# Running sum of the log decay by triangular matmul instead of a vector scan, with decay logits and values loaded token-major

## The chip, the cores and the metric

The kernel runs on one core of one Trainium2 chip. The metric is the device time of one execution, in microseconds (us). Engines are named as in the profile: PE (TensorE), PEld (its weight loads), DVE (VectorE), ACT (ScalarE), POOL (GpSimd), SP (SyncE, which here only issues DMAs).

## What is computed

A gated linear attention over 4 batches, 8 heads, 768 tokens and head size 48 feeds a mixture of 8 experts with a greedy, capacity-bound assignment, and that feeds a two-layer network with the nonlinearity h * cos(h). The change lies in the attention:

```python
f = 1.0 / (1.0 + np.exp(-f_logit))
for t in range(S):
    state = f[:, :, t, :, None] * state + np.einsum('bhd,bhe->bhde', k[:, :, t], v[:, :, t])
    y[:, :, t] = np.einsum('bhd,bhde->bhe', q[:, :, t], state)
```

## The kernel before

The program has three stages in a row: attention, a search of routing thresholds, and the experts with the two-layer network behind them. The attention stage takes the recurrence in chunks of 128 tokens. With 4 batches and 6 chunks there are 24 units u, u = 4 * chunk + batch. The 8 heads of a unit are held as 4 pairs; one head of a pair lies on partitions 0 to 47, the other on 64 to 111, and the rest is padding.

For a unit, `forget` makes l = ln(1 + exp(-f_logit)) on ACT, which is minus the log of the decay. `decay` makes its running sum A over the 128 tokens, on DVE, by one scan over 4 pairs x 128 tokens (L259); a second operand, `amask`, is 0 at each pair's first token, which restarts the sum, and a limit elsewhere. `scale` makes exp(A) and exp(-A) on ACT (L266, L267), the last column of the latter into G (L268), and scales keys and queries with them on POOL into kT (L270) and qT (L272). `turn` transposes kT on PE (L278). `scores` multiplies keys and queries on PE (L289), `cut` masks the scores on DVE (m, L293). `mix` adds state times queries (L303) and values times masked scores (L305) on PE and copies the sum to yT on ACT (L307). `outer` makes the chunk's own keys times values on PE (L316), `carry` adds them to the state on DVE (L326, L328), `fade` scales the state with G on POOL (L334). `gate` turns yT to token-major and makes the router logits in one product xl on PE (L341); ACT copies the rows out (L346), DVE sums the logits (L352). After every fourth unit `first_counts` runs a row of small DVE instructions (`best_expert`, L189 to L196, and L205) and four matmuls cn (L211), which start the search.

A loop over i spreads a unit over five turns: `at(k, f)` runs step f of unit i - k. Each engine keeps the order in which the program is written (`in_order`), so within a turn DVE runs carry, conversions, cuts, scan; PE runs xl, transposes, products, scores, outer products; ACT runs the copy of xl, the copy of the transposed keys, the exponentials, yT, and then the two activations of `forget`. Beside this, a generator converts the two-layer network's weights in 28 parts, about eight of its steps in each turn (`fill`): a load on SP (wr), an Abs on ACT (wv, L132), integer operations on DVE (L150, L152, L154, and w, L159), a rounding copy on ACT (wih and woh, L166), and a subtraction on DVE (L136).

Loads are issued on SP two turns ahead. q, k and f come together, feature-major, into one of three ring buffers (two DMAs of 48 partitions); v comes token-major, padded to 64 columns a head. `warm_up` runs bf16 matmuls on zeros at the end of turns 0 and 2 (18 and 12 of them).

The two tiles `cn0` and `tot` and the warming tile have a PSUM bank of their own (tag `sm`); with `w`, `tr`, `tk`, `sc0`, `sc1`, `y` and `kv` all eight banks are taken.

Of the kernel before, what the change touches and what calls it, by code (L numbers as in the profile page):

```python
# [9 lines left out]
F32 = mybir.dt.float32  # L10
# [3 lines left out]
AF = mybir.ActivationFunctionType  # L14
ALU = mybir.AluOpType
# [4 lines left out]
P = 128  # L20
B, H, S, D = 4, 8, 768, 48
HD = H * D
NCH = S // P
NU = B * NCH
NP = H // 2
E = 8
# [3 lines left out]
DECAY_LIMIT = 60.0  # L30
# [168 lines left out]
def first_counts(nc, wk, ps, K, Z, a, n):  # L199
    V = nc.vector  # L200
    s = slice(a, a + n)
    C = wk.tile([P, n, P], BF16, name="C0", tag="C0")

    def reach():
        V.tensor_tensor(C, Z["mx"][:, s, None].to_broadcast([P, n, P]), K["t0"].bitcast(F32)[:, None, :].to_broadcast([P, n, P]), op=ALU.is_ge)  # L205

    best_expert(nc, wk, K, Z["lg"][:, s], Z["mx"][:, s], Z["wm"][:, s], Z["oh"][:, s], n, reach)
    yield
    cn = ps.tile([P, E], F32, name="cn0", tag="sm")
    for c in range(n):  # L210
        nc.tensor.matmul(cn, C[:, c], Z["oh"][:, a + c], start=(c == 0), stop=(c == n - 1))  # L211
    if a == 0:
        V.tensor_copy(Z["cn"], cn)
    else:
        V.tensor_tensor(Z["cn"], Z["cn"], cn, op=ALU.add)
    yield


def attention(tc, nc, ctx, K, qkf, v64, xs, Z, G, wp, wg, win, wout, consts, late):
    V, SC, PE, GP = nc.vector, nc.scalar, nc.tensor, nc.gpsimd  # L220
    ap = ctx.enter_context(tc.tile_pool(name="at", bufs=1))
    wk = ctx.enter_context(tc.tile_pool(name="wk", bufs=2))
    ps = ctx.enter_context(tc.tile_pool(name="aps", bufs=1, space=PSUM))
    warm = ap.tile([P, 512], BF16, name="warm")
    V.memset(warm, 0.0)
    ring = [ap.tile([P, 3, NP, P], F32, name=f"ring{i}") for i in range(3)]
    for t in ring:
        V.memset(t[:, 2], 60.0)
        GP.memset(t[:, :2], 0.0)
    consts()  # L230
    amask = ap.tile([P, NP, P], F32, name="amask")
    V.memset(amask, DECAY_LIMIT + 2.0)
    V.memset(amask[:, :, 0:1], 0.0)
    st_all = [ap.tile([P, NP, P], F32, name=f"st{b}") for b in range(B)]
    for t in st_all:
        GP.memset(t, 0.0)
    st = {}

    def load(u):
        if u < NU:  # L240
            c, b = divmod(u, B)
            x = ring[u % 3]
            for a, z in ((2, 3), (0, 2)) if u == 0 else ((0, 3),):
                for j in range(2):
                    nc.sync.dma_start(x[64 * j:64 * j + D, a:z], qkf[b, c, j, :, a:z])
            v = wk.tile([P, H, 64], F32, name="v", tag="v", bufs=6)
            nc.sync.dma_start(v, v64[b, c * P:(c + 1) * P])
            st[u] = dict(x=x, v=v)

    def forget(u):  # L250
        x = st[u]["x"]
        uu = wk.tile([P, NP * P], F32, name="uu", tag="uu", bufs=1)
        SC.activation(uu, x[:, 2].rearrange("p a t -> p (a t)"), AF.Exp, scale=-1.0)
        SC.activation(uu, uu, AF.Ln, bias=K["ones"][:, 0:1])
        st[u]["l"] = uu

    def decay(u):
        A = st[u]["A"] = wk.tile([P, NP, P], F32, name="A", tag="A")
        V.tensor_tensor_scan(A.rearrange("p a t -> p (a t)"), amask.rearrange("p a t -> p (a t)"), st[u].pop("l"), 0.0, op0=ALU.min, op1=ALU.add)  # L259

    def scale(u):
        d = st[u]
# [33 lines left out]
    def mix(u):  # L296
        c, b = divmod(u, B)
        d = st[u]
        T, v = st_all[b], d["v"]
        y = ps.tile([P, NP, P], F32, name="y", tag="y")  # L300
        for p in range(NP):
            if c > 0:
                PE.matmul(y[:, p], T[:, p], d["qT"][:, p], start=True, stop=False)  # L303
            for j in range(2):
                PE.matmul(y[64 * j:64 * j + 64, p], v[:, 2 * p + j], d["sc"][j][:, p], start=(c == 0), stop=True)  # L305
        yT = d["yT"] = wk.tile([P, NP, P], F32, name="yT", tag="yT")
        SC.copy(yT, y)  # L307

    def outer(u):
        if u // B < NCH - 1:  # L310
            d = st[u]
            kv = d["kv"] = ps.tile([P, NP, D], F32, name="kv", tag="kv")
            for p in range(NP):
                for j in range(2):
                    h = 2 * p + j
                    PE.matmul(kv[64 * j:64 * j + D, p], d["kk"][:, p, 64 * j:64 * j + D], d["v"][:, h, :D], start=True, stop=True)  # L316

    def carry(u):
        c, b = divmod(u, B)
# [38 lines left out]
            yield from first_counts(nc, wk, ps, K, Z, u - n + 1, n)  # L358

    def warm_up(n):  # L360
        w = ps.tile([P, 512], F32, name="wp", tag="sm")
        for _ in range(n):
            PE.matmul(w, warm[:, :P], warm, start=True, stop=True)

# [16 lines left out]
    for i in range(NU + 5):  # L381
        def at(k, f, *a):
            if 0 <= i - k < NU:
                f(i - k, *a)

        def fill(n):
            for _ in range(n):
                next(conv, None)
        counts, gates = gates, gate(i - 4) if 0 <= i - 4 < NU else iter(())
        if i > NU:  # L390
            next(tail, None)
        at(4, carry)
        next(gates, None)
        at(2, turn)
        at(1, scale)
        F = (3, 2, 3) if i > 1 else (0, 0, 0)
        fill(F[0])
        at(3, mix)
        at(0, forget)
        next(counts, None)  # L400
        next(gates, None)
        fill(F[1])
        at(2, scores)
        fill(F[2])
        at(2, cut, 0)
        at(2, cut, 1)
        at(0, decay)
        next(gates, None)
        at(4, fade)
        at(3, outer)  # L410
        fill(0 if i < NU else 3)
        if i < len(WARM) and WARM[i]:
            warm_up(WARM[i])
        if i == 0:
            turning()
        load(i + 2)
# [433 lines left out]


@with_exitstack
def kernel(ctx, tc, qkf, v64, qkvf, wg, wcat, win, wout, out):
    nc = tc.nc
    V = nc.vector
    cp = ctx.enter_context(tc.tile_pool(name="cp", bufs=1))
# [18 lines left out]
    def late(ps):  # L875
# [1 line left out]
        cnt = cp.tile([P, 1], F32, name="cnt")  # L877
        V.tensor_scalar(ok, G.rearrange("p a b -> p (a b)"), math.exp(-DECAY_LIMIT), 0.0, op0=ALU.is_ge, op1=ALU.add, accum_out=cnt)
        yield
        tot = ps.tile([1, 1], F32, name="tot", tag="sm")  # L880
        nc.tensor.matmul(tot, cnt, K["ones"][:, 0:1], start=True, stop=True)
        V.tensor_copy(flag, tot)
        yield
# [2 lines left out]

    with ExitStack() as actx:
        with in_order(tc, nc):
            R = attention(tc, nc, actx, K, qkf, v64, xs, Z, G, wp, wg, win, wout, consts, late)
    with ExitStack() as fctx:  # L890
        sp = fctx.enter_context(tc.tile_pool(name="sp", bufs=1))
        pools = recurrence_pools(tc, fctx)
# [9 lines left out]
        experts(tc, nc, ectx, K, R, Z, xs, wcat, out)  # L902


_INS = ["qkf", "v64", "qkvf", "wg", "wcat", "win", "wout"]
_OUTS = [((B * S, HD), "float32")]


def layout(q, k, v, f_logit, moe_w_gate, moe_w1, moe_w2, moe2_w_in, moe2_w_out):
# [2 lines left out]
    tok = [a.transpose(0, 2, 1, 3).reshape(B, S, HD) for a in (q, k, v, f_logit)]  # L912
    w1 = moe_w1.reshape(E, 3, P, F1 // P, P).transpose(0, 2, 3, 1, 4).reshape(E, P, F1 // P, HD)
    w2 = moe_w2.reshape(E, F1 // P, P, HD).transpose(0, 2, 1, 3)
    dmaj = [a.reshape(B, NP, 2, NCH, P, D).transpose(0, 3, 2, 5, 1, 4) for a in (q, k, f_logit)]
    got = {
        "qkf": np.stack(dmaj, 4), "v64": np.pad(v.transpose(0, 2, 1, 3), ((0, 0), (0, 0), (0, 0), (0, 64 - D))), "qkvf": np.stack(tok, 2), "wg": moe_w_gate, "wcat": np.concatenate([w1, w2], 3),
        "win": moe2_w_in, "wout": moe2_w_out,
    }
    got = {n: np.ascontiguousarray(a) for n, a in got.items()}  # L920
# [24 lines left out]
```

## Time and profile before

| What | us |
|---|---|
| Median of 3 runs | 911.61 |
| Lowest and highest run | 911.2, 913.1 |
| Span of the profiled execution, from first to last instruction | 909.6 |
| PE busy, share of the span | 828.2, 91% |
| DVE busy | 648.3, 71% |
| ACT busy | 371.4, 41% |
| POOL busy | 394.4, 43% |

The profiled execution's own time is not listed apart from the three runs; its span of 909.6 us is 1.6 us under the lowest of them and 2.0 us under the median. The shares are means over stages with different limits, so what matters is read by stage. Matmuls are pipelined and their ends are modelled: PE's pace is read from start to start. In rows in order of time, the bracket at the end holds the idle time before the instruction and what ended it; x is how many instructions a row merges, and an fp32 matmul has two records. In rows of a group, the two numbers behind the bar are busy us and mean ns of one.

### The profile page before, as it was taken

How to read it: one execution, taken by the hardware profiler on the slowest of the kernel's cores; microseconds unless marked ns; L12 is line 12 of the kernel's file. 1: busy time of each engine (PE TensorE's matmuls, PEld its weight loads, DVE VectorE, ACT ScalarE, POOL GpSimd, SP SyncE). 2: the span in 40 equal slices, each digit the busy share in tenths (PEclk: the TensorE clock that was granted, in tenths of full speed). 3: DMA queues.
4: the chain of work that ended last, by engine and by line, in shares of the span. 5: the costliest groups of instructions: out<-in, count | busy, mean ns of one | idle time of the engine just before them, and what ended most of it. 6: DMA issues, size and time to landing. Idle time of an engine off the chain costs nothing.

```text
span 909.6 us, 15391 instructions
## 1 busy us (share of the span) xinstructions
PE 828.2 (91%) x5672; PEld 753.7 (83%) x5674; DVE 648.3 (71%) x1521; ACT 371.4 (41%) x686; POOL 394.4 (43%) x326
## 2 busy tenths in 40 slices
PE   6688889885399999999999999999999999999996
PEld 3566657664299998998999899989989999999996
DVE  7899999997657946975695588469756945653453
ACT  4646656551133352343235233423532352533332
POOL 4444544440341472365138324723651474634133
PEclk9889999987589999999999999999999999999999
DMA  8987777820320230122013002301220133200000
GB/s 198 232 200 193 184 186 174 197 83 28 102 67 1 79 107 8 53 54 87 1 53 114 27 1 79 113 3 53 62 78 1 53 114 90 74 29 27 1 1 27
DMA packets 27331, 73.45 MB, mean 81 GB/s; under 512 B 4624, under 2 KB 7696, under 8 KB 27248
## 3 DMA queue, kind: packets, MB, share of 16 engines
q1 hardware_dynamic: 24176, 62.95, 26.1%
q0 software_dynamic: 3072, 9.44, 3.2%
q8 instruction: 46, 0.75, 0.3%
q14 instruction: 37, 0.30, 0.1%
HBM read 62.94 MB, written 9.44 MB: 80 GB/s over the span
## 4 chain that ended last, share of the span: by engine, by line
PE 66%; DVE 5%; issue 1%; DMA 1%; POOL 0%; SPq 0%; POOLq 0%; ACT 0%; DVEq 0%
PE pC L698 7%; PE accD L761 7%; PE pC L699 7%; PE accD L763 7%; PE pC L700 7%; PE accD L762 7%; PE pA L698 4%; PE pA L699 3%; PE accB L698 3%; PE pA L700 3%; PE accB L699 3%; PE accB L700 3%; DVE C L508 2%; PE cn L504 1%; DVE thr L556 1%; DVE thr L548 1%
## 5 line engine op out<-in xcount | busy, mean ns | idle before, releaser
L751 POOL TENSOR_TENSOR gl<-g,gh 128x384 fp32r<-128x384 f32 x128 | 134.5, 1052 | 266.2 <-ACT gh L750 263.2
L681 POOL TENSOR_TENSOR wl<-raw,wh 128x768 fp32r<-128x768 f32 x64 | 118.2, 1853 | 41.1 <-ACT wh L680 40.5
L761 PE MATMUL accD<-woh,gh 128*128 128x384 f32 x384 | 131.0, 341 | 0.0
L763 PE MATMUL accD<-woh,gl 128*128 128x384 f32 x384 | 130.4, 340 | 0.5 <-POOL gl L751 0.5
L700 PE MATMUL pC<-yTh,wil 128*128 128x384 f32 x384 | 130.1, 339 | 0.0
L762 PE MATMUL accD<-wol,gh 128*128 128x384 f32 x384 | 129.4, 337 | 0.0
L699 PE MATMUL pC<-yTl,wih 128*128 128x384 f32 x384 | 129.4, 337 | 0.0
L698 PE MATMUL pC<-yTh,wih 128*128 128x384 f32 x384 | 129.0, 339 | 0.0
L745 ACT ACTIVATE fr<-fr,halfpi 128x384 f32<-128x384 f32 x128 | 78.8, 616 | 105.2 <-DVE fr L744 97.6
L747 DVE TENSOR_TENSOR g<-pC,fr 128x384 f32<-128x384 f32 x128 | 71.0, 555 | 61.8 <-ACT fr L745 55.0
L750 ACT CAST gh<-g 128x384 fp32r<-128x384 f32 x128 | 65.8, 514 | 112.8 <-DVE g L747 99.8
L742 DVE TENSOR_SCALAR ki<-pC 128x384 int32<-128x384 f32 x128 | 70.8, 553 | 20.6 <-PE pC L700 19.8
L690 DVE SCALAR_TENSOR_TENSOR hl<-pA,hh 128x384 fp32r<-128x384 f32 x64 | 35.5, 555 | 65.4 <-ACT hh L689 65.2
L270 POOL TENSOR_TENSOR kT<-ring,em 128x512 f32<-128x512 f32 x24 | 33.1, 1381 | 104.8 <-ACT em L266 104.8
L680 ACT CAST wh<-raw 128x768 fp32r<-128x768 f32 x64 | 52.6, 833 | 62.8 <-DMA raw<-in_wcat_dram 29.6
L689 ACT ACTIVATE hh<-pA 128x384 fp32r<-128x384 f32 x64 | 31.5, 492 | 112.6 <-PE pA L700 112.6
L763 PEld LDWEIGHTS accD<-woh,gl 128*128 128x128 f32 x384 | 72.0, 188 | 1.6 <-POOL gl L751 1.1
L744 DVE SCALAR_TENSOR_TENSOR fr<-pC,ki 128x384 f32<-128x384 f32 x128 | 71.1, 556 | 3.1
L699 PEld LDWEIGHTS pC<-yTl,wih 128*128 128x128 f32 x384 | 72.1, 188 | 0.5 <-DVE yTl L693 0.5
L761 PEld LDWEIGHTS accD<-woh,gh 128*128 128x128 f32 x384 | 72.1, 188 | 0.1
L762 PEld LDWEIGHTS accD<-wol,gh 128*128 128x128 f32 x384 | 72.2, 188 | 0.0
L700 PEld LDWEIGHTS pC<-yTh,wil 128*128 128x128 f32 x384 | 72.1, 188 | 0.1
(178 smaller groups left out, 1818.9 us busy)
## 6 DMA issues: line engine op xcount, KB each, us to landing
raw<-in_wcat_dram SPq DMA_DIRECT2D x64, 384.0 KB, 3.3
ring<-in_qkf_dram SPq DMA_DIRECT2D x46, 288.0 KB, 5.8
v<-in_v_dram SPq DMA_DIRECT2D x24, 256.0 KB, 6.2
wr<-in_win_dram SPq DMA_DIRECT2D x12, 512.0 KB, 5.4
wr<-in_wout_dram SPq DMA_DIRECT2D x16, 384.0 KB, 3.5
xs<-xx SPq DMA_DIRECT2D x24, 192.0 KB, 5.4
ring<-in_qkf_dram SPq DMA_DIRECT2D x2, 192.0 KB, 3.6
xg<-xs,idx POOLq DMA_INDIRECT x24
```

The source lines that it names most:

```text
L681: GP.tensor_tensor(l, raw, h.bitcast(F32), op=ALU.subtract)
L698: PE.matmul(o, ah, bh, start=first, stop=False)
L699: PE.matmul(o, ah, bl, start=False, stop=False)
L700: PE.matmul(o, al, bh, start=False, stop=last)
L742: V.tensor_scalar(ki, p, INV2PI, 0.25, op0=ALU.mult, op1=ALU.add)
L744: V.scalar_tensor_tensor(fr, p, INV2PI, ki, op0=ALU.mult, op1=ALU.subtract)
L745: SC.activation(fr, fr, AF.Sin, bias=halfpi, scale=TWO_PI)
L747: V.tensor_tensor(g, p, fr, op=ALU.mult)
L751: GP.tensor_tensor(gl, g, gh.bitcast(F32), op=ALU.subtract)
L761: PE.matmul(r["accD"][t], gh[:, s], R["oh"][:, f], start=(f == 0), stop=False)
L762: PE.matmul(r["accD"][t], gh[:, s], R["ol"][:, f], start=False, stop=False)
L763: PE.matmul(r["accD"][t], gl[:, s], R["oh"][:, f], start=False, stop=(f == NF - 1))
```

## The change

The running sum moves from DVE to PE: with l token-major, four fp32 matmuls per unit (one for each pair, l as weights, the 0/1 triangle `mask` as the moving operand) give A feature-major in PSUM. f is therefore loaded token-major, together with v, which loses its padding: one DMA of 128 partitions from the token-major array that the fallback path had already. The ring buffers hold q and k alone. For unit 0 f is loaded first, then q and k, then v. `logs` are two padded tiles whose padding stays 0. The limit that `amask` put on A is gone. The products with v are 48 instead of 64 columns wide, and the padding rows of their PSUM tile are zeroed once. A takes the bank `sm`; what was in it moves to the bank of `kv`. `decay` is called at the end of a turn, behind `outer`, and ahead of the warming matmuls.

```diff
-    cn = ps.tile([P, E], F32, name="cn0", tag="sm")
+    cn = ps.tile([P, E], F32, name="cn0", tag="kv")
...
-    ring = [ap.tile([P, 3, NP, P], F32, name=f"ring{i}") for i in range(3)]
+    ring = [ap.tile([P, 2, NP, P], F32, name=f"ring{i}") for i in range(3)]
     for t in ring:
-        V.memset(t[:, 2], 60.0)
-        GP.memset(t[:, :2], 0.0)
+        GP.memset(t, 0.0)
+    logs = [ap.tile([P, NP, 2, 64], F32, name=f"logs{i}") for i in range(2)]
+    for t in logs:
+        V.memset(t, 0.0)
+    yps = ps.tile([P, NP, P], F32, name="y", tag="y")
+    V.memset(yps, 0.0)
     consts()
-    amask = ap.tile([P, NP, P], F32, name="amask")
-    V.memset(amask, DECAY_LIMIT + 2.0)
-    V.memset(amask[:, :, 0:1], 0.0)
...
-            for a, z in ((2, 3), (0, 2)) if u == 0 else ((0, 3),):
-                for j in range(2):
-                    nc.sync.dma_start(x[64 * j:64 * j + D, a:z], qkf[b, c, j, :, a:z])
-            v = wk.tile([P, H, 64], F32, name="v", tag="v", bufs=6)
-            nc.sync.dma_start(v, v64[b, c * P:(c + 1) * P])
-            st[u] = dict(x=x, v=v)
+            vf = wk.tile([P, 2, HD], F32, name="vf", tag="vf", bufs=6)
+            src = qkvf[b, c * P:(c + 1) * P, 2:4]
+            if u == 0:
+                nc.sync.dma_start(vf[:, 1], src[:, 1])
+            else:
+                nc.sync.dma_start(vf, src)
+            for j in range(2):
+                nc.sync.dma_start(x[64 * j:64 * j + D], qk[b, c, j])
+            if u == 0:
+                nc.sync.dma_start(vf[:, 0], src[:, 0])
+            st[u] = dict(x=x, v=vf[:, 0].rearrange("t (h d) -> t h d", h=H), f=vf[:, 1])
 
     def forget(u):
-        x = st[u]["x"]
-        uu = wk.tile([P, NP * P], F32, name="uu", tag="uu", bufs=1)
-        SC.activation(uu, x[:, 2].rearrange("p a t -> p (a t)"), AF.Exp, scale=-1.0)
-        SC.activation(uu, uu, AF.Ln, bias=K["ones"][:, 0:1])
-        st[u]["l"] = uu
+        uu = wk.tile([P, NP, 2, D], F32, name="uu", tag="uu", bufs=1)
+        SC.activation(uu.rearrange("t p j d -> t (p j d)"), st[u]["f"], AF.Exp, scale=-1.0)
+        SC.activation(logs[u % 2][:, :, :, :D], uu, AF.Ln, bias=K["ones"][:, 0:1])
 
     def decay(u):
-        A = st[u]["A"] = wk.tile([P, NP, P], F32, name="A", tag="A")
-        V.tensor_tensor_scan(A.rearrange("p a t -> p (a t)"), amask.rearrange("p a t -> p (a t)"), st[u].pop("l"), 0.0, op0=ALU.min, op1=ALU.add)
+        A = st[u]["A"] = ps.tile([P, NP, P], F32, name="A", tag="A")
+        for p in range(NP):
+            PE.matmul(A[:, p], logs[u % 2][:, p].rearrange("t j d -> t (j d)"), K["mask"], start=True, stop=True)
...
-                PE.matmul(y[64 * j:64 * j + 64, p], v[:, 2 * p + j], d["sc"][j][:, p], start=(c == 0), stop=True)
+                PE.matmul(y[64 * j:64 * j + D, p], v[:, 2 * p + j], d["sc"][j][:, p], start=(c == 0), stop=True)
...
-        w = ps.tile([P, 512], F32, name="wp", tag="sm")
+        w = ps.tile([P, 512], F32, name="wp", tag="kv")
...
         at(2, cut, 1)
-        at(0, decay)
         next(gates, None)
         at(4, fade)
         at(3, outer)
+        at(0, decay)
         fill(0 if i < NU else 3)
         if i < len(WARM) and WARM[i]:
             warm_up(WARM[i])
```

On PE, between one turn's last scores and the next turn's products, with a state (sc are the scores, kv the outer products, tk the transposed keys, st the state), the order before was

```order
L289 MATMUL sc_664<-qT,kT 128x128
L316 MATMUL kv<-v,kk 48x48 x8
L341 MATMUL xl<-turn,yT 128x104 x4
L278 MATMUL tk<-ident,kT 128x128 x4
L303 MATMUL y<-qT,st_138 128x128
L305 MATMUL y<-m,v 64x128 x2
```

and is now

```order
L294 MATMUL sc_679<-qT,kT 128x128
L321 MATMUL kv<-vf,kk 48x48 x8
L264 MATMUL A<-mask,logs_93 128x128 x4
L346 MATMUL xl<-turn,yT 128x104 x4
L283 MATMUL tk<-ident,kT 128x128 x4
L308 MATMUL y<-qT,st_138 128x128
L310 MATMUL y<-m,vf 48x128 x2
```

Four matmuls of A stand between the outer products and the next turn's xl; all else keeps its place.

On DVE, around the cuts of a turn (m) and the carry of the next (st), the order before was

```order
L293 TENSOR_TENSOR m<-sc_407,mask 128x512
L293 TENSOR_TENSOR m<-sc_408,mask 128x512
L259 SCALAR_TENSOR_TENSOR A<-amask,uu 128x512
L328 COPY st_138<-kv 48x4x48 x2
L152 TENSOR_SCALAR wv<-wv 128x512
L154 SCALAR_TENSOR_TENSOR wv<-wr,wv 128x512
```

and is now

```order
L298 TENSOR_TENSOR m<-sc_416,mask 128x512
L298 TENSOR_TENSOR m<-sc_417,mask 128x512
L333 COPY st_138<-kv 48x4x48 x2
L152 TENSOR_SCALAR wv<-wv 128x512
L154 SCALAR_TENSOR_TENSOR wv<-wr,wv 128x512
```

The scan is gone from between them, and the carry follows the cuts.

## Rows read from the trace of the kernel before

**Rows 1.** Page, DVE's busy tenths in 40 slices of the span.
```profile
DVE  7899999997657946975695588469756945653453
```

**Rows 2.** Stretches: length, PE, PEld, DVE, ACT, POOL busy (instructions), PEclk, DMA share, GB/s.
```profile
45.99:196.00 150.01, 126.53 (x1204) 95.42 (x1202) 146.69 (x240) 89.60 (x181) 71.11 (x54) 0.90 0.73 180
...
131.97:138.16 6.19, 6.19 (x39) 4.29 (x39) 5.97 (x15) 3.90 (x8) 3.57 (x3) 0.51 0.69 183
...
250.00:909.60 659.60, 642.14 (x3927) 617.48 (x3927) 424.44 (x1080) 245.41 (x435) 291.23 (x235) 0.99 0.16 50
```

**Rows 3.** Waits, 0 to 230 us: who waited for whom, us in total, times, longest.
```profile
POOL kT L270 <- ACT em L266: 104.8, 24, 8.5
PEld y L305 <- DVE m L293: 27.7, 36, 2.4
ACT em L266 <- DVE A L259: 25.7, 17, 3.7
...
ACT wih L166 <- DVE w L159: 13.6, 7, 2.9
```

**Rows 4.** Groups by line on DVE, 45.99 to 197.22 us.
```profile
L259 DVE TENSOR_TENSOR_SCAN A<-amask,uu 128x512 f32<-128x512 f32 x19 | 23.1, 1214 | 0.0
```

**Rows 5.** PE in order of time, one step: start us, us, instruction, count.
```profile
110.46 1.16 PE L289 MATMUL sc<-qT,kT 64*128 64x128 f32 x16
111.55 0.56 PE L316 MATMUL kv<-v,kk 128*48 128x48 f32 x16
112.05 1.14 PE L341 MATMUL xl<-turn,yT 128*128 128x104 f32 x8
113.02 0.60 PE L278 MATMUL tk<-ident,kT 128*128 128x128 f32 x4
113.46 0.39 PE L303 MATMUL y<-qT,st 128*128 128x128 f32 x2
...
115.23 0.49 PE L303 MATMUL y<-qT,st 128*128 128x128 f32 x2
115.65 0.44 PE L305 MATMUL y<-m,v 128*64 128x128 f32 x4
116.02 0.49 PE L303 MATMUL y<-qT,st 128*128 128x128 f32 x2
```

**Rows 6.** ACT in the same step, in order of time.
```profile
110.58 0.58 ACT L307 COPY yT<-y 128x512 f32<-128x512 f32 x1 [1.32 <-PE y L305]
...
111.72 0.72 ACT L254 ACTIVATE uu<-uu,ones 128x512 f32<-128x512 f32 x1
```

**Rows 7.** DVE in order of time: first of a count, and the carry behind.
```profile
132.60 0.16 DVE L189 TENSOR_REDUCE mx<-lg 128x4 f32<-128x32 f32 x1
...
134.79 0.71 DVE L326 TENSOR_TENSOR st<-st,kv 48x192 f32<-48x192 f32 x2
```

**Rows 8.** PE and DVE in order of time, head of the program.
```profile
1.28 6.27 PE L363 MATMUL wp<-warm 128*128 128x512 bf16 x18 [1.28 <-DVE warm L225]
...
16.10 0.43 DVE L150 TENSOR_SCALAR wv<-wv 128x512 f32<-128x512 f32 x1 [1.87 <-ACT wv L132]
```

**Rows 9.** DVE, three conversions in time; three lines' shortest, median, longest (ns).
```profile
125.53 1.21 DVE L150 TENSOR_SCALAR wv<-wv 128x384 f32<-128x384 f32 x1
126.78 1.31 DVE L152 TENSOR_SCALAR wv<-wv 128x384 int32<-128x384 int32 x1
128.12 1.17 DVE L154 SCALAR_TENSOR_TENSOR wv<-wr,wv 128x384 int32<-128x384 int32 x1
...
L150 DVE TENSOR_SCALAR wv<-wv x28: 344/428/1495, 16.1 to 206.6; 128x384 f32<-128x384 f32 x16, 128x512 f32<-128x512 f32 x12
L152 DVE TENSOR_SCALAR wv<-wv x28: 359/887/1383, 16.6 to 207.0; 128x384 int32<-128x384 int32 x16, 128x512 int32<-128x512 int32 x12
L154 DVE SCALAR_TENSOR_TENSOR wv<-wr,wv x28: 548/693/1805, 18.0 to 207.4; 128x384 int32<-128x384 int32 x16, 128x512 int32<-128x512 int32 x12
```

**Rows 10.** PE in order of time, the wait before its clock fell.
```profile
131.01 0.43 PE L305 MATMUL y<-m,v 128*64 128x128 f32 x2 [1.79 <-DVE m L293]
```

More of the change, by code (lines that the diff above doesn't have):

```diff
@@ L216, in first_counts, with attention @@
     yield
-def attention(tc, nc, ctx, K, qkf, v64, xs, Z, G, wp, wg, win, wout, consts, late):
+def attention(tc, nc, ctx, K, qk, qkvf, xs, Z, G, wp, wg, win, wout, consts, late):
     V, SC, PE, GP = nc.vector, nc.scalar, nc.tensor, nc.gpsimd
@@ L299, in mix @@
         T, v = st_all[b], d["v"]
-        y = ps.tile([P, NP, P], F32, name="y", tag="y")
+        y = yps
         for p in range(NP):
@@ L315, in outer @@
                     h = 2 * p + j
-                    PE.matmul(kv[64 * j:64 * j + D, p], d["kk"][:, p, 64 * j:64 * j + D], d["v"][:, h, :D], start=True, stop=True)
+                    PE.matmul(kv[64 * j:64 * j + D, p], d["kk"][:, p, 64 * j:64 * j + D], d["v"][:, h], start=True, stop=True)
     def carry(u):
@@ L852, with kernel @@
 @with_exitstack
-def kernel(ctx, tc, qkf, v64, qkvf, wg, wcat, win, wout, out):
+def kernel(ctx, tc, qk, qkvf, wg, wcat, win, wout, out):
     nc = tc.nc
@@ L879, in late @@
         yield
-        tot = ps.tile([1, 1], F32, name="tot", tag="sm")
+        tot = ps.tile([1, 1], F32, name="tot", tag="kv")
         nc.tensor.matmul(tot, cnt, K["ones"][:, 0:1], start=True, stop=True)
@@ L888 @@
         with in_order(tc, nc):
-            R = attention(tc, nc, actx, K, qkf, v64, xs, Z, G, wp, wg, win, wout, consts, late)
+            R = attention(tc, nc, actx, K, qk, qkvf, xs, Z, G, wp, wg, win, wout, consts, late)
     with ExitStack() as fctx:
@@ L902 @@
         experts(tc, nc, ectx, K, R, Z, xs, wcat, out)
-_INS = ["qkf", "v64", "qkvf", "wg", "wcat", "win", "wout"]
+_INS = ["qk", "qkvf", "wg", "wcat", "win", "wout"]
 _OUTS = [((B * S, HD), "float32")]
@@ L914, in layout @@
     w2 = moe_w2.reshape(E, F1 // P, P, HD).transpose(0, 2, 1, 3)
-    dmaj = [a.reshape(B, NP, 2, NCH, P, D).transpose(0, 3, 2, 5, 1, 4) for a in (q, k, f_logit)]
+    dmaj = [a.reshape(B, NP, 2, NCH, P, D).transpose(0, 3, 2, 5, 1, 4) for a in (q, k)]
     got = {
-        "qkf": np.stack(dmaj, 4), "v64": np.pad(v.transpose(0, 2, 1, 3), ((0, 0), (0, 0), (0, 0), (0, 64 - D))), "qkvf": np.stack(tok, 2), "wg": moe_w_gate, "wcat": np.concatenate([w1, w2], 3),
+        "qk": np.stack(dmaj, 4), "qkvf": np.stack(tok, 2), "wg": moe_w_gate, "wcat": np.concatenate([w1, w2], 3),
         "win": moe2_w_in, "wout": moe2_w_out,
```

## The prediction

> **What bounds the kernel now.** I read the slices of the page first, then the stretches, then the waits, then one step in time. In the slices of 22.7 us each, VectorE (DVE) stands at 9 from the second to the ninth and falls off behind that [rows 1]: that is the attention stage, the only one that the change touches. The stretches give numbers [rows 2]: between the scan that starts at 45.99 us and the one at 196.00 lie 18 steps (19 scans, the group in [rows 4]), so a step takes 150.01 / 18 = 8.33 us. DVE is busy for 146.69 us of it, 8.15 us a step or 97.8%. PE is busy for 126.53 at a mean granted clock of 0.90, ACT for 89.60, POOL for 71.11. From 250 us on, in the experts, PE is busy for 642.14 of 659.60 us, and nothing in that stretch is edited.
>
> The waits say the same from the other side [rows 3]: PE's weight loads wait for the masked scores m of DVE (27.7 us), ACT for A from the scan (25.7 us) and for w of the weight conversion (13.6 us). No wait of that length has DVE as the one that waits. What DVE sheds in this stage is therefore time, until another engine's own work per step is reached. The question is how close that is.
>
> **The change, part by part.**
>
> *The scan goes.* In these 18 steps it costs 23.1 / 19 = 1.21 us each [rows 4]. DVE's work falls from 8.15 to 6.94 us a step, and at the same 97.8% a step that only DVE bounds would take 7.09.
>
> *Four matmuls a step come to PE.* First PE's own work, from a step at the full clock [rows 5]: scores 1.09 us (110.46 to 111.55), outer products 0.50, xl 0.97, transposes 0.44, and four pairs of state and score product of 0.79 each (115.23 to 116.02), 3.16: together 6.16. The trace has no fp32 matmul with the triangle. The nearest below is the transpose, 128x128 against 128 columns, 0.44 us for four; the nearest above is the state product L303, 0.42 us each (115.23 to 115.65), 1.68 for four, which sits between matmuls of another tile shape. I take xl, 0.97 us: it too is four fp32 matmuls in a row with 128x128 weights, with two records each, only with 104 columns for 128. PE then needs 6.16 + 0.97 = 7.13 us (6.60 to 7.84 by the ends), still below 8.33, but no longer with room.
>
> *A wait comes with them.* The matmul of step u needs the logarithm of step u, and ACT takes Exp and Ln only after the copy yT, which needs the last product on PE. Today yT starts at 110.58, and Ln runs from 111.72 to 112.44 [rows 6]. Both activations shrink from 512 to 384 columns, together by at most a quarter of twice 0.72, 0.36 us; I take 0.2, since part of each is fixed: the end is 112.24. PE is through with the outer products at 112.05 [rows 5]. So it waits some 0.2 us in each step, and xl, transposes and the products of the next step are queued behind that. The loop from product to yT, logarithm, matmul and next product takes 7.13 + 0.2 = 7.33 us. ACT itself has 89.60 us of work in 150 and bounds nothing; that em and ep now read from PSUM is taken as nothing.
>
> *The steps that count.* After every fourth step DVE runs best_expert in a row, from 132.60 to the carry at 134.79, 2.19 us [rows 7]. Averaged that is 0.55, so DVE has 6.39 us in a plain step and 8.58 in a counting one, 8.77 with the same 2.2% idle. PE bounds the plain steps and DVE the counting ones. The masks can be late by the length of the new matmul without PE noticing, but ACT's rounding copies, too, wait for DVE ahead of yT, so I credit no carry-over: (3 x 7.33 + 8.77) / 4 = 7.69 us. With full carry-over it would be 7.33.
>
> *The head.* The first matmul of A now stands before the 18 warming matmuls on PE, which ran from 1.28 us for 6.27 [rows 8]. It must wait for the first load and logarithm, so warming ends later by that much, and the first transposes are behind it. The cover is DVE's first conversion, which starts only at 16.10, after 1.87 us of waiting for ACT's wv; ACT copies the transposed keys before it takes wv, so if they come late, up to 2 us are lost. On the other side five scans leave the first 46 us, worth 6.1 us if DVE bounded there; but it idles there for first loads, and of what is shed I expect to keep no more than the head loses. I put it at 0, with a gain of 3 us (half the scans) and a loss of 2 us as its ends.
>
> *Edits with one answer.* Per step the load shrinks from 2 x 288 + 256 = 832 KB to 2 x 192 + 384 = 768 KB in as many DMAs, while the DMA share is 0.73 [rows 2]: 0. If that cover went, loads would bound; at 7.69 us a step the share would be 0.73 x 8.33 / 7.69 = 0.79, so it stays. On SP's queue the load of v and f now stands ahead of q and k and needs a buffer that was released a step earlier: 0. The forget gate no longer waits for the ring buffer that POOL releases: 0, since it is loaded two steps ahead. Products of 48 instead of 64 columns stream the same 128: 0. Counts, warming and the flag move to the bank of kv, where outer must wait for the addition of the counts on DVE; that lies in the counting step, whose lateness is already charged. The memsets of the head lie before DVE has work: 0.
>
> *Sum.* (8.33 - 7.69) x 18 = 11.5 us less: the span goes from 909.6 to 898.1. The median of the runs, 911.61, is 2.0 us above the profiled span, and I keep that: 900.1 us.
>
> **Rule against row: DVE beside POOL.** DVE's conversions stretch where POOL works. The three at 125.53 to 129.2 take 1.21, 1.31 and 1.17 us, against shortest ones of 0.344, 0.359 and 0.548: 2.44 us lost in that step [rows 9]. The scan hardly does (19 of them average 1.214 us [rows 4]), because POOL waits for it: kT waits for em, and em for A [rows 3]. So a stretch in which DVE was safe from POOL goes, and the conversions may lose more. The Trainium skill (SBUF — State Buffer, Who interferes with whom) gives the reason: DVE and GpSimd share a port pair under an exclusive lock, and a DVE instruction with two SBUF inputs or in a two-port mode fully blocks, or is blocked by, a GpSimd instruction that reads SBUF. The trace agrees as far as those stretched rows go. By the rule the freed time would partly go to POOL; rival 4 is that case.
>
> **The rivals.**
>
> 1. *Better, 889 to 894.* Counting steps are absorbed, because the masks have the new matmul's length as slack: 7.33 a step, 18.0 us less, 893.6. If the matmul costs the lower end of 0.44 and DVE alone bounds, 7.09 a step, 22.3 less, 889.3. For it speaks that plain steps leave DVE almost 1 us; against it that ACT waits for DVE's w today [rows 3].
>
> 2. *No change, about 911.* PE loses its clock. After a wait of 1.79 us for m [rows 10] PE's clock fell: from 131.97 to 138.16 it was granted 0.51 [rows 2], the 1.2 GHz level. Three product pairs, the counts and the scores took 6.19 us there; at the full clock they are 3 x 0.79 + 0.2 + 1.09 = 3.66. A fall costs 2.5 us, which is harmless while DVE bounds and counts in full once PE does. DVE is late by 8.77 - 7.33 = 1.4 us in a counting step; if each of these makes the clock fall, a step is 7.69 + 2.5 / 4 = 8.32 us. Against it: the waits for m come 36 times, up to 2.4 us long [rows 3], with a mean clock of 0.90 [rows 2], so most of them cost no clock; and PE will be busier than now.
>
> 3. *Slower, about 923.* The same mechanism, with PE's wait for the logarithm as second place: where a rounding copy stands ahead of yT on ACT and waits for DVE (13.6 us over 7 copies, 1.9 each [rows 3]), Exp, Ln and the matmul are late by as much, and PE idles long enough. If half the steps lose the clock: 7.69 + 1.25 = 8.94, or 11 us more, 922.6. It decides from one fall in four steps, (8.33 - 7.69) / 2.5.
>
> 4. *Slower, about 917, by the port.* If all of POOL's 71.11 / 18 = 3.95 us a step fell on conversions, 1.51 more than in the step shown would be lost: DVE 6.94 + 1.51 = 8.45, 8.64 at 97.8%, 5.6 us more. Against it: the cuts read PSUM and never stretch, and they and the carries can lie beside POOL as well.
>
> **How the numbers follow.** About 0.2% (1.8 us) is what a measurement can tell from no change. The forecast, 7.5 to 8.1 us a step, gets 0.52; rival 1 gets 0.24; rival 2, with a gain lost otherwise, 0.10; rivals 3 and 4 get 0.09 and 0.05. That the change does not do what it says is excluded by the order: the scans are gone from DVE. Faster is then 0.52 + 0.24 = 0.76, same 0.10, slower 0.14. The range goes from rival 1's lower part, 890, past no change to 913; rival 3, 4's far end and the last of rival 1 are outside, under 0.2.
>
> **What would show it.** Right: no scan on DVE; the step from one matmul of A to the next about 7.7 us between the same steps; DVE's share below 95% in it, with its idle time ahead of the cuts; PE's clock above 0.95; A's matmuls 0.9 to 1.2 us for four, with a short wait for Ln ahead of them; counting steps longer than the others; the experts' stretch as long as before. Wrong: long waits of PE for Ln with rows at half clock behind them (rivals 2, 3), or conversions on DVE that stretch further with DVE still at 98% (rival 4).

## The result, and the profile after

The changed kernel takes 885.07 us, the median of four runs (883.84 to 887.28), against 911.4 for the kernel before on the same chip: a ratio of 0.9715, 95% interval 0.9695 to 0.9735. A second set of runs of the same code gave 887.31 us (0.9738, interval 0.9724 to 0.9752). The forecast was 900.1, range 890 to 913: the sign was right, the gain of 26 us is more than twice the 11.5 forecast, and the result is below the range. The profiled span falls from 909.6 to 882.1 us, by 27.5.

The page of the kernel after, its slices of 22.05 us each (PEclk is PE's granted clock in tenths of full speed). DVE's row answers to [rows 1]; its high stretch now ends in the eighth slice instead of the ninth. (Before, its nines begin in the third slice, not in the second as the prediction reads them; nothing hangs on it.)

```profile
PE   6889999953999999999999999999999999999996
...
DVE  6999999975679558846974696479557845652553
...
PEclk9999999975899999999999999999999999999999
```

The stretches answer to [rows 2]. First the kernel after, then the kernel before in the same windows (columns: window, length, busy us and instructions of PE, PEld, DVE, ACT and POOL, granted clock, DMA share, GB/s):

```profile
12.00:24.00 12.00, 8.83 (x97) 6.49 (x95) 8.05 (x13) 7.29 (x16) 4.45 (x4) 1.00 1.05 261
24.00:36.00 12.00, 10.13 (x136) 8.94 (x136) 11.03 (x20) 9.80 (x22) 6.58 (x6) 1.00 0.95 286
36.00:48.00 12.00, 9.97 (x104) 8.28 (x106) 11.71 (x19) 8.13 (x18) 8.86 (x7) 1.00 0.82 245
40.00:170.00 130.00, 123.91 (x1338) 97.38 (x1338) 124.47 (x221) 83.49 (x181) 70.36 (x54) 1.00 0.63 192
```

```profile
12.00:24.00 12.00, 9.12 (x81) 6.00 (x80) 9.47 (x12) 7.35 (x15) 4.16 (x4) 0.86 1.04 252
24.00:36.00 12.00, 8.06 (x69) 7.16 (x70) 9.65 (x16) 7.02 (x14) 3.54 (x3) 0.72 1.04 246
36.00:48.00 12.00, 8.36 (x82) 6.50 (x80) 11.81 (x18) 7.87 (x17) 6.25 (x5) 0.81 0.85 208
40.00:170.00 130.00, 106.98 (x1041) 80.54 (x1036) 127.11 (x209) 79.24 (x161) 63.65 (x48) 0.91 0.75 184
```

From 40 to 170 us both engines are busy for 95% of the time, PE 123.91 and DVE 124.47 of 130, and PE's clock is full (1.00) throughout. Before, DVE had 127.11 and PE 106.98, part of that at the lower clock.

Where the time went is read best from the scores, which start once per unit; I number them s0 to s23. These starts are read from PE in order of time:

| Start of scores, us | s0 | s1 | s4 | s23 | s1 to s4 | mean of 19 steps, s4 to s23 |
|---|---|---|---|---|---|---|
| before | 12.57 | 21.66 | 48.03 | 206.87 | 26.37 | 8.36 |
| after | 12.88 | 21.96 | 39.95 | 179.45 | 17.99 | 7.34 |

Of 27.5 us, 8.1 are gained by s4 (48.03 - 39.95, the head), and 19.3 in the 19 steps behind it (158.84 - 139.50). From s23 to the end both kernels take 702.7 us.

One step on PE after, in order of time, answers to [rows 5]:

```profile
73.95 1.16 PE L264 MATMUL A<-mask,logs 128*128 128x128 f32 x8 [0.17 <-ACT logs L259]
74.94 1.04 PE L346 MATMUL xl<-turn,yT 128*128 128x104 f32 x8
75.82 0.60 PE L283 MATMUL tk<-ident,kT 128*128 128x128 f32 x4
76.25 0.39 PE L308 MATMUL y<-qT,st 128*128 128x128 f32 x2
...
79.25 1.16 PE L294 MATMUL sc<-qT,kT 64*128 64x128 f32 x16
80.34 0.56 PE L321 MATMUL kv<-vf,kk 128*48 128x48 f32 x16
81.08 1.16 PE L264 MATMUL A<-mask,logs 128*128 128x128 f32 x8 [0.17 <-ACT logs L259]
...
88.20 1.16 PE L264 MATMUL A<-mask,logs 128*128 128x128 f32 x8
```

The four matmuls of A take 0.99 us to the next instruction (73.95 to 74.94), and PE waits 0.17 for Ln (`logs`) ahead of them. The step is 81.08 - 73.95 = 7.13 us, and 7.12 to the next.

The waits (0 to 230 us) answer to [rows 3]:

```profile
POOL kT L275 <- ACT em L271: 78.8, 24, 5.5
...
PE A L264 <- ACT logs L259: 10.1, 19, 2.8
...
PEld y L310 <- DVE m L298: 3.8, 7, 1.2
```

PE's weight loads waited 27.7 us for the masks before and wait 3.8 now; ACT's 25.7 us for the scan are gone. The count, DVE in order of time, answers to [rows 7]:

```profile
52.77 0.18 DVE L189 TENSOR_REDUCE mx<-lg 128x4 f32<-128x32 f32 x1
...
54.13 0.19 DVE L196 TENSOR_TENSOR oh<-w,wm 128x32 bf16<-128x32 f32 x1
54.24 0.71 DVE L331 TENSOR_TENSOR st<-st,kv 48x192 f32<-48x192 f32 x2
```

From the first reduction to the carry it is 1.47 us, against 2.19 before; so it is in three of the five counts. In the other two (112.42 and 169.74 us) it is 2.22 as before:

```profile
112.42 0.18 DVE L189 TENSOR_REDUCE mx<-lg 128x4 f32<-128x32 f32 x1
...
113.78 0.93 DVE L196 TENSOR_TENSOR oh<-w,wm 128x32 bf16<-128x32 f32 x1
```

The difference is `oh` (L196), and it goes with POOL. Beside the 0.93 us POOL runs this:

```profile
113.34 1.32 POOL L275 TENSOR_TENSOR kT<-ring,em 128x512 f32<-128x512 f32 x1 [3.52 <-ACT em L271]
```

`oh` ends at 114.71, kT at 114.66. Where `oh` takes 0.19 us (54.13, 83.33, 140.70) POOL is idle, and before, where it takes 0.92 or 0.93 in all five counts, it lies beside kT in each.

### The profile page after: what moved, and what is told of

Its sections match the earlier page's. It is cut to its first block, busy times and chain, and to the rows that moved or that the text cites. A ratio compares the mean times of both kernels' runs of the same rounds, so it can differ in the third digit from the quotient of the medians.

```text
span 882.1 us, 15725 instructions
## 1 busy us (share of the span) xinstructions
PE 824.7 (93%) x5866; PEld 757.0 (86%) x5866; DVE 615.7 (70%) x1495; ACT 363.8 (41%) x686; POOL 393.5 (45%) x326
## 4 chain that ended last, share of the span: by engine, by line
PE 68%; DVE 6%; issue 1%; POOL 1%; DMA 1%; POOLq 0%; ACT 0%; DVEq 0%
PE pC L703 8%; PE accD L766 8%; PE pC L704 7%; PE accD L768 7%; PE pC L705 7%; PE accD L767 7%; PE pA L703 4%; PE pA L704 3%; PE accB L703 3%; PE pA L705 3%; PE accB L704 3%; PE accB L705 3%; DVE C L513 1%; PE cn L509 1%; DVE thr L561 1%; DVE thr L553 1%
## 5 line engine op out<-in xcount | busy, mean ns | idle before, releaser
L703 PEld LDWEIGHTS pC<-yTh,wih 128*128 128x128 f32 x384 | 72.0, 188 | 0.1
```

The source lines that it names most:

```text
L703: PE.matmul(o, ah, bh, start=first, stop=False)
```

## The experiments

In the expectations, W is the theory that the gain is DVE's work (the scan's time), C that it is PE's clock, which more work on PE holds up; N that a counting step is charged in full, as forecast, S that the other steps' slack absorbs it; B that fewer loaded bytes made the head faster, O that the order on the load queue did. Ratios are to the kernel before on the same chip. The changed kernel's own two medians lie 2.2 us apart, so differences of about 2 us between variants are not used.

**The scan back, beside the matmuls** (on the changed kernel, onto a tile that nobody reads, behind the cuts):

```diff
+    def scan(u):
+        l = logs[u % 2].rearrange("t p j d -> t (p j d)")
+        V.tensor_tensor_scan(idle, l, l, 0.0, op0=ALU.min, op1=ALU.add)
...
         at(2, cut, 1)
+        at(0, scan)
```

> The changed kernel with a scan of the old size put back on DVE at its old place, its result unused; the matmuls still make A. Theory W (the step is the larger of two engines' own work: DVE 6.94 us without the scan, 8.15 with it, PE 7.13): the step from one matmul of A to the next goes from 7.29 back to about 8.3 us, and with the first turns the kernel to 903 to 911 us. Theory C (most of the gain is PE's clock, which no longer falls, and the loads and warming of the head): the scan costs little, 885 to 893 us.

Measured: 909.96 us, 0.9988 (0.9978 to 0.9999). Nearly the whole gain is gone, though PE has the same instructions as after. The steps s4 to s23 take 8.44 us. From 40 to 170 us, in this kernel:

```profile
40.00:170.00 130.00, 114.58 (x1156) 90.88 (x1156) 124.43 (x208) 71.88 (x156) 59.11 (x45) 0.93 0.61 179
```

DVE is as busy as in the changed kernel, PE less and at a lower clock. But s4 starts at 42.65 and s1 to s4 takes 21.13 us, 5.2 less than before: part of the head's gain isn't DVE's time for the scan.

**No running sum at all** (on the kernel before: l is taken for A, so the output is not the reference's):

```diff
-        uu = wk.tile([P, NP * P], F32, name="uu", tag="uu", bufs=1)
+        uu = wk.tile([P, NP * P], F32, name="uu", tag="uu", bufs=3)
...
-        A = st[u]["A"] = wk.tile([P, NP, P], F32, name="A", tag="A")
-        V.tensor_tensor_scan(...)
+        st[u]["A"] = st[u].pop("l").rearrange("p (a t) -> p a t", a=NP)
```

> The kernel before with the scan taken out and nothing in its place: the log decay itself stands for its running sum, so the output is not the reference's. Loads, warming and PE's work are those of before. Theory W: DVE's 6.94 us and PE's 6.16 leave a step of about 7.1 us, 880 to 888 us in all; what it is under the changed kernel's 885 is the price of the new matmuls. Theory C: the clock still falls and the head is as before, 900 to 908 us.

Measured: 887.48 us, 0.9744 (0.9727 to 0.9761), steps of 7.28 us. Taking the scan away brings what the change brings; the four matmuls then cost nothing net. Its s4 starts at 44.27, though, between before (48.03) and after (39.95).

**The matmuls of A twice** (`for p in 2 * list(range(NP))` in `decay`):

> The changed kernel with the four matmuls of A issued twice, to the same place. Theory W: PE bounds now, so the step goes from 7.29 by the price of four such matmuls, 0.97 us, to about 8.2, 18 to 22 us more, 903 to 907 us. If DVE still bounds: under 5 us more. Theory C: no more than 3 us, since PE only gets busier.

Measured: 901.48 us, 0.9902 (0.9885 to 0.9918), 16.4 more than after for 24 x 0.99 = 23.8 us of PE work; steps of 7.89; W had expected 903 to 907. Now PE bounds alone:

```profile
40.00:170.00 130.00, 126.78 (x1393) 103.67 (x1390) 100.77 (x205) 79.22 (x173) 63.29 (x51) 1.00 0.64 192
```

and among its waits (0 to 230 us) DVE waits for PE:

```profile
DVE m L298 <- PE sc L294: 14.4, 11, 3.1
```

So PE's room, 2.17 us a step before (8.33 - 6.16 by the forecast's figures), is used up once the four matmuls are there and the step is shorter.

**Unused matmuls beside the scan** (on the kernel before: four fp32 matmuls onto bank `sm`, at the place where A's stand after):

```diff
+    def beside(u):
+        w = ps.tile([P, NP, P], F32, name="wq", tag="sm")
+        for p in range(NP):
+            PE.matmul(w[:, p], K["ident"], K["mask"], start=True, stop=True)
```

> The kernel before with four fp32 matmuls of the same shape added behind the outer products, on constants, their result unused. Theory W: PE has room beside DVE's 8.15 us, so the time stays at 911 within 3 us. Theory C: PE is busier, its clock falls less often (mean 0.90 before), and the kernel gains 8 us or more, 895 to 903.

Measured: 911.17 us, 1.0006 (0.9994 to 1.0018).

```profile
40.00:170.00 130.00, 115.33 (x1157) 90.34 (x1156) 127.09 (x211) 78.58 (x158) 62.69 (x48) 0.96 0.74 183
```

PE's clock rises from 0.91 to 0.96 with the work, and the time stays. C falls: while DVE bounds, PE's clock is worth nothing in the end. (s4 starts 1.9 us earlier, at 46.17; in the time nothing of that is left.)

**The count twice** (on the changed kernel, `best_expert` issued a second time onto tiles that nobody reads; the counts' matrix C, which it also makes, is written a second time in its own place, so the count on PE waits for the second row):

> The changed kernel with the row of small DVE instructions behind every fourth step (best_expert and the comparison C) issued twice, the second time to scratch tiles: some 1.5 us more for DVE in each of five full counting steps, 1.2 in two half ones at the end. Theory N (no carry-over, as predicted: PE bounds the plain steps, DVE the counting ones): each shows in full, 7 to 9 us more, 892 to 894 us. Theory S (the masks and the new matmul's length are slack that spreads a late step over the next ones): under 4 us more, 885 to 889 us.

Measured: 898.26 us, 0.9853 (0.9827 to 0.9879), more than either theory allowed. Its steps s4 to s23 average 7.86 us, 9.9 us more in all. PE in order of time shows why, behind its second count:

```profile
96.09 0.71 PE L325 MATMUL kv<-vf,kk 128*48 128x48 f32 x16 [1.61 <-DVE cn L219]
96.73 2.08 PE L268 MATMUL A<-mask,logs 128*128 128x128 f32 x8
98.60 1.59 PE L350 MATMUL xl<-turn,yT 128*128 128x104 f32 x8
```

The outer products waited 1.61 us for the counts' addition in the bank they now share, and behind that A takes 2.08 us for 1.16 at the full clock; the granted clock from 96.00 to 97.70 us is 0.60. That is the mechanism of rival 2, a wait of PE with a fall of its clock behind it. At the first count it came by another way, the one of rival 3: A waits for Ln, not for the bank, and from 62 to 66 us the granted clock is 0.53:

```profile
63.51 2.08 PE L268 MATMUL A<-mask,logs 128*128 128x128 f32 x8 [1.65 <-ACT logs L263]
```

It doesn't come at every count. Around the first, two steps take 9.45 and 11.17 us (7.44 and 8.47 after), around the second 7.68 and 10.14 (7.31 and 7.01); at the third and fourth no step is over 7.4, and at the fifth one takes 8.34 (6.97). For the single count, S is read from the changed kernel itself, below; this run alone does not decide it.

**Warming first, less warming.** Two runs on the changed kernel look for the head's gain in the warming matmuls: one puts them ahead of A, the other shortens them (`WARM = (10, 0, 4)` for `(18, 0, 12)`).

> The changed kernel with the warming matmuls ahead of the first and third matmul of A, as far as the order of the kernel before allows. If the gain of the first turns came from the new order of warming (the clock rises later but holds): 2 us or more slower, 887 to 890 us. If it came from DVE's lighter load and the loads' order: 885 within 1.5 us.

> The changed kernel with 10 and 4 warming matmuls in place of 18 and 12. They stand ahead of the second matmul of A (11.46 us, its logarithm done at 9.89) and of the second transposes (20.42 us, their keys done at 15.41). If the head is on the path: 1 to 3 us faster, 882 to 884 us. If DVE's work from its first conversion on sets the end and the loads set that: 885 within 1 us; if the clock falls for it: slower.

Measured: 883.71 us (0.97, interval 0.9676 to 0.9724) and 885.38 (0.9702, 0.9679 to 0.9726). Neither matters.

**q and k ahead of v and f in every unit, the first too** (on the changed kernel):

```diff
-            if u == 0:
-                nc.sync.dma_start(vf[:, 1], src[:, 1])
-            else:
-                nc.sync.dma_start(vf, src)
             for j in range(2):
                 nc.sync.dma_start(x[64 * j:64 * j + D], qk[b, c, j])
-            if u == 0:
-                nc.sync.dma_start(vf[:, 0], src[:, 0])
+            nc.sync.dma_start(vf, src)
```

> The changed kernel with q and k loaded ahead of v and f in every unit, the first too, as in the kernel before. If the gain of the first turns came from the early f: the first logarithm and the first turns come 2 us or more later, and so does the end, 887 to 890 us. If it came from DVE: 885 within 1.5 us.

Measured: 890.62 us, 0.9759 (0.9732 to 0.9787). s0 starts at 18.43 instead of 12.88, and as much is in the time (890.62 against 885.07). The expectation speaks of the order of the kernel before, which is inexact: that one, too, loads f of unit 0 first. What is shown is the price of a late first f, not a source of the gain.

**v unpadded alone** (on the kernel before: 192 KB of v for 256, products of 48 columns):

> The kernel before with only the load of v changed: 192 KB token-major without padding in place of 256 KB, products 48 wide, scan and all else as before. If the first turns are bounded by the DMA engines (share 1.04 from 12 to 36 us, ACT waiting 5.9 us there for weights): the scores of the fifth unit come 2 to 5 us earlier than 48.0 us and the kernel gains 1 to 4 us, 907 to 910. If they are bounded by DVE: 911 within 1 us.

Measured: 910.12 us, 0.9993 (0.9983 to 1.0003); s4 at 46.24, 1.8 us earlier, of which nothing measurable is left at the end.

**More bytes, and the buffers.** The first of two runs loads k token-major with v and f (192 KB more per unit) and has four buffers where six don't fit:

> The changed kernel with k loaded a second time, token-major beside v and f, unused: 192 KB more for each unit, four buffers for six. If the DMA engines bound the first turns: the fifth unit's scores come 3 to 6 us later than 39.95 us, and the end as much later, 888 to 891 us. If DVE and PE bound them too: 885 within 1.5 us.

Measured: 914.92 us, 1.0052 (1.0033 to 1.0072), far from what was expected. Its queue of loads (SP's waits) shows another cause than bytes:

```profile
SPq L249 <- PE kv L321: 120.1, 20, 11.2
```

20 loads wait for the outer products to release a buffer, 6 us each, with everything on SP behind them. The second run therefore loads 128 KB more per unit onto two tiles of their own, and leaves the six buffers:

```diff
+            more = wk.tile([P, 256], F32, name="more", tag="more", bufs=2)
+            nc.sync.dma_start(more, qkvf[b, c * P:(c + 1) * P, 1, :256])
```

> The changed kernel, with 128 KB more loaded per unit (256 columns of k), onto two tiles of its own that nobody reads, so that six buffers of v and f stay and no load waits longer for a buffer: the earlier load of more with its four buffers cost 28 us. If that was the buffers, this costs what theory B charges for twice 64 KB and no more: 885 to 893 us. If it was the bytes, in the plain steps too, it costs two thirds of the 28 us: 900 to 906 us.

Measured: 886.74 us, 0.9732 (0.9712 to 0.9752). These bytes cost nothing (DMA share 0.76 for 0.63 from 40 to 170 us). So the 28 us of the first run (914.92 against 887.31) go, by SP's waits, to the buffers; the 64 KB by which it loads more than the second were not tried apart.

**The changed kernel again, and without POOL's fade** (the call of `fade` left out):

> The changed kernel once more, on the same chip as its variants: 885 within 1.5 us.

> The changed kernel without fade, the POOL instruction that scales the state (1.12 us a step): the output is not the reference's. It takes no step from PE or DVE, but its hold on the port that DVE's conversions need. If PE's own 7.13 us bound the steps: 883 to 886 us. If DVE's conversions, stretched by POOL, bound them as much: 4 us or more faster, 875 to 881 us.

Measured: 887.31 us (0.9738), 2.2 above the first set where 1.5 was expected, and 881.94 (0.9673, interval 0.9655 to 0.9692), between the two expectations. Without the fade, which makes the output wrong, the steps s4 to s23 fall from 7.34 to 7.16 us, 3.5 in all, and two groups of conversions on DVE shrink. Groups by line, 40 to 170 us, first with the fade (the changed kernel again):

```profile
L150 DVE TENSOR_SCALAR wv<-wv 128x384 f32<-128x384 f32 (+1 forms) x20 | 19.3, 964 | 0.2
...
L152 DVE TENSOR_SCALAR wv<-wv 128x384 int32<-128x384 int32 (+1 forms) x20 | 17.6, 881 | 0.6
```

and without it:

```profile
L150 DVE TENSOR_SCALAR wv<-wv 128x384 f32<-128x384 f32 (+1 forms) x20 | 13.6, 679 | 0.2
L152 DVE TENSOR_SCALAR wv<-wv 128x384 int32<-128x384 int32 (+1 forms) x21 | 13.1, 622 | 0.6
```

The plain step stays (7.13, from A at 76.22 to A at 83.35), so the gain lies in the other steps. What stands between the changed kernel's mean step (7.34) and PE's own loop (7.13) is then, by these groups, mostly DVE stretched by POOL; this is argued and not shown, since the run also takes fade out of the chain to the state.

**What of the loads made the head faster.** The bytes back alone, onto tiles of their own (64 KB more per unit, as before); the order alone (q and k first from unit 1 on); and that order with the scan back:

> The changed kernel, with 64 KB more loaded per unit behind v and f (128 columns of k, onto tiles that nobody reads), so that a unit loads 832 KB again as in the kernel before; the result is the same. If the fewer bytes (theory B) make the first turns faster, the fifth scores start 3 to 5 us later than in the changed kernel (near 43 to 45 us) and the time is 888 to 891 us. If it is the order on the load queue (theory O), the fifth scores start within 1.8 us of the changed kernel's 39.95 us (1.8 us is what the unpadded v alone, which has the same bytes as the change, gained there) and the time is 885 to 888.

> The changed kernel, with q and k ahead of v and f on the load queue from unit 1 on, as f stood behind POOL's release of the ring buffer before; unit 0 as in the changed kernel. Theory O: the fifth scores start 3 to 4 us later than in the changed kernel (43 to 44 us) and the time is 888 to 890 us. Theory B: no difference, the fifth scores near 40 us and 885 to 887 us.

> The changed kernel with a scan back on VectorE in every turn (onto a tile that nobody reads) and with q and k ahead of v and f from unit 1 on. With the scan back alone the fifth scores started at 42.65 us, 5.4 us ahead of the kernel before, and the time was 910.0 us. Theory O: the fifth scores start at 46 to 48 us again. Theory B: they stay at 42 to 44. The whole time tells little, since DVE bounds the steps behind: 909 to 914 either way.

Measured: 887.36 us (0.9734, interval 0.9718 to 0.975), 887.53 (0.9734, 0.9718 to 0.975) and 911.03 (0.9997, 0.9986 to 1.0008). The starts of the scores, with those of the other kernels:

| Start of scores, us | s1 | s4 | s1 to s3 | s3 to s4 | s1 to s4 |
|---|---|---|---|---|---|
| before | 21.66 | 48.03 | 16.40 | 9.97 | 26.37 |
| before, v unpadded | 21.08 | 46.24 | 15.21 | 9.95 | 25.16 |
| before, unused matmuls | 21.71 | 46.17 | 15.38 | 9.08 | 24.46 |
| before, no running sum | 21.28 | 44.27 | 17.02 | 5.97 | 22.99 |
| scan back | 21.52 | 42.65 | 12.67 | 8.46 | 21.13 |
| scan back, q and k first | 24.66 | 45.35 | 12.06 | 8.63 | 20.69 |
| after | 21.96 | 39.95 | 12.05 | 5.94 | 17.99 |
| after, run again | 23.35 | 41.33 | 12.05 | 5.93 | 17.98 |
| bytes back | 24.12 | 42.11 | 12.04 | 5.95 | 17.99 |
| q and k first | 24.66 | 42.64 | 12.04 | 5.94 | 17.98 |

Neither B nor O is told apart by the time: both end where the changed kernel run again does (887.31). Bytes and order move s1 by up to 3 us, but s1 of the unchanged code moves by 1.4 too. From s1 to s4 they change nothing: 17.98 or 17.99 us in all four kernels that have the sum on PE and no scan.

## Why the prediction was right in sign and wrong in size

*Right.* DVE's work bound the stage: put back alone, it takes the gain away. A costs 0.99 us (0.97 forecast) with 0.17 of waiting for Ln (0.2 forecast). The clock is at 1.00, as "above 0.95" said, and rivals 2 and 3 did not come; the doubled count shows that the mechanism of both is real, once the counts are twice as long. The part behind s23 is unchanged. Rival 4 did not come either: the four conversions' means sum to 3.53 us in the kernel before (L150, L152, L154 and L159 from 40 to 170 us: 775 + 883 + 1075 + 794 ns) and to 3.58 after in the same window (965 + 881 + 857 + 875). From 36 us on it is 3.63:

```profile
L150 DVE TENSOR_SCALAR wv<-wv 128x384 f32<-128x384 f32 (+1 forms) x21 | 20.8, 990 | 0.2
L152 DVE TENSOR_SCALAR wv<-wv 128x384 int32<-128x384 int32 (+1 forms) x21 | 19.0, 904 | 0.6
L159 DVE SCALAR_TENSOR_TENSOR w<-wr,wv 128x384 int32<-128x384 int32 (+1 forms) x21 | 18.4, 875 | 0.6
L154 DVE SCALAR_TENSOR_TENSOR wv<-wr,wv 128x384 int32<-128x384 int32 (+1 forms) x21 | 18.0, 857 | 0.6
```

(36 to 170 us, the kernel after.) These means mix tiles of 512 and 384 columns; for those of 384 alone the sum goes from 3.26 to 3.53 us (40 to 170 us). POOL's blocking moved to other conversions; it did not grow by the 1.5 us a step of that rival. The Trainium skill (SBUF — State Buffer, Who interferes with whom) states that DVE and GpSimd share a port pair under an exclusive lock. The traces agree: without the fade L150 goes from 964 to 679 ns, and `oh`, 0.19 us alone, takes 0.93 beside kT and ends with it.

*The first term that failed: the mean step, above all the steps that count.* "I credit no carry-over" put a counting step at 8.77 us and the mean at 7.69; it is 7.34. A's starts show it. The count at 81.97 us lies in the step from 81.08 to 88.20, 7.12 us, no longer than a plain one; that at 139.34 in one of 7.13 (138.77 to 145.90), and that at 112.42 in steps of 7.49 and 7.35. Only the first, at 52.77, costs much: 8.27 (51.04 to 59.31). So the masks' slack carries over nearly in full, as in rival 1's first branch. Two things made the slack larger than I granted: DVE has 6.39 us of work in a plain step (the forecast's own figure) of 7.13, and three of the five counts are 0.7 us shorter, because `oh` (L196) doesn't lie beside POOL's kT there. The first does most of it: the count at 112.42 has its full length of 2.22 us and costs 0.6 us over two steps, where 1.4 was charged. The reason I gave against it, that ACT's rounding copies wait for DVE, was true and without effect: ACT waits 16.5 us for w in 11 copies, and yT is not late by it in the steps shown. This term is 19 x (7.69 - 7.34) = 6.7 us.

Not all of it is carry-over. The plain step was mis-sized too: 7.33 forecast, 7.13 measured, with the wait of 0.17 inside it. The product pairs take 3.00 us (76.25 to 79.25) for 3.16, and xl 0.88 (74.94 to 75.82) for 0.97. By the forecast's own formula, a plain step of 7.13 makes the mean (3 x 7.13 + 8.77) / 4 = 7.54. So 2.9 of the 6.7 us are the plain step, and 3.8 the counting steps. That the mean of 7.34 falls on rival 1's 7.33 is in part luck: the plain step is 0.20 shorter than its sum says, and the long steps at the start (9.13 from s4 to s5, and those at the first count) put back 0.21.

*The second: the head.* I put it at 0 with a gain of 3 as its end; it is 8.1, or 6.7 by the second profile of the same code (s4 at 41.33). With the scan back it falls by 2.7 to 3.1 (17.99 against 21.13 and 20.69 from s1 to s4), just the 3 us that I named and then cancelled against the late warming; but the warming runs show that its place and length cost nothing. The other 5.2 us (26.37 to 21.13) I had not seen. The table of starts divides them. From s1 to s3 the gain is 4.35 us (16.40 to 12.05), and it isn't the running sum on DVE: without any sum, but with the old loads, these two steps take 17.02, and with the scan back, but the new loads, 12.67 and 12.06. ACT's waits in the head (8 to 46 us) show what left; first before, then with no running sum, then after:

```profile
ACT wv L132 <- DMA wr<-in_win_dram: 5.9, 2, 3.2
ACT em L266 <- DVE A L259: 5.8, 4, 3.6
```

```profile
ACT wv L132 <- DMA wr<-in_win_dram: 6.1, 3, 2.9
```

```profile
ACT wv L132 <- DMA wr<-in_win_dram: 1.0, 1, 1.0
```

Before, ACT stood twice between s1 and s3 for weights of the two-layer network that had not landed (2.69 and 3.17 us), with yT and the exponentials behind that in its queue:

```profile
25.74 0.66 ACT L132 ACTIVATE wv<-wr 128x512 f32<-128x512 f32 x1 [2.69 <-DMA wr<-in_win_dram]
...
31.80 0.66 ACT L132 ACTIVATE wv<-wr 128x512 f32<-128x512 f32 x1 [3.17 <-DMA wr<-in_win_dram]
```

Without the sum it still does; with the new loads it waits once, 1.0 us after and 1.8 with the scan back, and not at all with q and k first besides. The 4.8 us less of waiting fit the 4.35 gained; that they are its cause is read from the queue's order and not shown by a run of its own. The step from s3 to s4 is the other way round: 9.97 before, 5.97 without a sum, 5.94 after, 8.46 and 8.63 with the scan back. There DVE's work for the sum is worth 2.5 to 2.7 us; the 1.3 to 1.5 left to 9.97 may be ACT's wait for the scan behind DVE's queue or PE's clock, and no run tells these apart. PE's clock is a rival for the head as a whole: granted 0.72 and 0.81 before (24 to 36 and 36 to 48 us), 1.00 after. With the unused matmuls it stands at 1.00 and 0.94, and s1 to s4 takes 24.46: beside the scan and the old loads it is worth some 1.9 of the 8.4 us, and no run shows it without them. Why the weights land earlier stays open: bytes and order are excluded from s1 on, v alone gives 1.2 (26.37 to 25.16) with 4.6 us of that wait left, and f apart from the ring buffer was not tried without the new sum.

*The sum.* Forecast 11.5 us in 18 steps; measured 27.5. The difference of 16.0 is 8.1 from the head, 3.8 from the counting steps, 2.9 from the plain ones, 0.6 from the nineteenth step, and 0.6 of rounding and of the steps before (8.36 for 8.33).

*A sign that misled.* "DVE's share below 95%" was to show the forecast right. It is 95.7% (124.47 of 130), with only 1.3 us of waiting for the scores, though the plain step is PE's. DVE's busy time includes the time that POOL blocks it (`oh` counts as 0.93 us beside kT and as 0.19 alone).

## What to carry to other kernels

When work moves from one engine to another, write down each engine's own work per step and take the larger mean first. Charge a periodic long step in full only where the next engine has nothing left to work on meanwhile; otherwise ask for how many steps the buffers between them cover it. Price the first turns on their own: here ACT stood 5.9 us there for loads that had not landed, which no mean of the later steps shows, and the change removed most of that without aiming at it. A bank that is shared after the change can be harmless with room to spare and still cost 3.5 us at one count once that room is used: double the holder's work once to see how far the edge is.

## What the runs showed of the hardware that was not expected

VectorE's busy time is elastic. The same instructions per step take 124.47 us of 130 in the changed kernel, 7.0 us a step at 7.3, and 100.77 with A's matmuls doubled, 6.1 us a step at 7.89; in the latter PE holds the step, and the conversions L150 and L152 take 612 and 616 ns for 965 and 881 (40 to 170 us). A busy share of 95% therefore doesn't say that DVE is the bound; the cuts waiting for the scores (4.9 us without the fade, 1.3 with it) say more. Without the fade:

```profile
L298 DVE TENSOR_TENSOR m<-sc,mask 128x512 f32<-128x512 f32 x38 | 24.3, 681 | 4.9 <-PE sc L294 4.9
```

And a wait of 1.61 us on PE was followed by rows at half speed (A 2.08 us for 1.16, granted clock 0.60 from 96.00 to 97.70), while the waits of 0.17 us, one in most steps, and one of 1.13 us in the changed kernel left the granted clock at 1.00 (40 to 170 us):

```profile
59.31 1.16 PE L264 MATMUL A<-mask,logs 128*128 128x128 f32 x8 [1.13 <-ACT logs L259]
```
